# GpSimd and SyncE's queue in program order, and the values' outputs in the scores' banks: a transformer block with cached attention on one core

## Chip, cores and metric

The kernel runs on one core of one Trainium2 chip. The metric is the device time of one execution in microseconds; the median of three runs of the kernel before is 3133.72 us (3131.37 to 3137.28).

## What is computed

A block with two halves over a sequence of 2048 rows of 576 numbers, all in float32. A small vector c gives six modulation vectors (shift, gain and gate for each half).

```python
h = layernorm(x) * (1 + ca) + sa
x = x + ga * A(h)        # attention: q = h @ wq, 32 query heads of 128, 16 key/value heads
                         # k, v: the last 512 positions of two caches; softmax(q k / sqrt(128)) v, then @ wo
h = layernorm(x) * (1 + cb) + sb
x = x + gb * B(h)        # (silu(h @ w1) * (h @ w3)) @ w2, inner width 4608
```

## The kernel before

**Precision.** A matrix that goes into a matmul is split into a high half, which ScalarE casts (`fp32r`), and a low half, which another engine subtracts (`split`, L82, its lines L84 and L85). A product is then three matmuls: high by high, high by low, low by high. Low halves of weights (`wl`, `vl`, `o`) are subtracted by GpSimd (POOL in the profile), those that come from PSUM (`ql`, `ptl`, `otl`) by VectorE.

**Attention.** The sequence lies in four blocks of 512 rows (`acc`, four tiles of 128 rows each). The work is a list of 128 slots: a half of the sequence, a head, a block. The loop over slots has four steps t for each slot i, and each step issues in this order: `turn(i-1, t)` transposes a tile of the exponentials (`pt`, ScalarE's copy `pth`); `scores(i, t)` makes a tile of scores `pss`, its maximum `nm`, the low half `ptl` of the slot before, and the exponential `p`; `query(i+1, t)` does a quarter of the projection `pq` of the next slot (in the last quarter `qh` and `ql` are split off); `attend_out(i-2, t)` multiplies by `wo` and adds into `acc`; then `run(i, t)` issues the tasks that were put down for this step. After the four steps `values(i-1)` issues twelve matmuls into `po` and splits them into `oth` and `otl`. On TensorE a step is 4 + 3 + 3 + 6 matmuls (two more in the last), and `values` 12.

**Tasks.** `at(i, t, ...)` puts loads and preparations into the list of a step. For a head whose first slot is i: `load_in` (L215, L217) loads its query weights at (i-3, 1), `split_in` (L223) makes `wh` and `wl` at (i-2, 1); `load_out` (L229) loads its rows of `wo` at (i-2, 1), `gate` (L779) multiplies them by the gate on GpSimd at (i-1, 0), `split_out` (L234) splits them at (i-1, 2); the caches are loaded by `load_kv` (L239), and `split_v` (L245) stands at (i-1, 0). Three buffers (`raw`) serve all these loads.

**Weights of the second half.** Its products are done by a scheme with seven products for a 2 x 2 block of tiles, so sums and differences of weight tiles are made ahead, during the attention, split, and stored to DRAM. `load_raw` (L478, L481) loads a set, `make_set` (L490 to L499) is called seven times for it, one item a step; `load_rows` (L526) and `make_rows` (L545 to L550 in an opening call four steps ahead, then seven items through `keep`, L532 to L536) do the same for `w2`. Five items fall on four steps in the stretches where this is done. A set is loaded six steps before its first item, a pair of rows seven steps before its opening call.

**Second half.** `mlp` runs over 72 groups of seven products (L577); in each it loads the next group's weights (L570) and interleaves the matmuls of the group pair before (`down`, L643, L653, rows loaded at L565).

**PSUM.** Eight banks: `E` (two), `T` (two, later given to a second output), tag `A` (two) for `pq`, `po` and later `py`, tag `S` (two) for `pss` and later `px`.

**Order.** TensorE, VectorE and ScalarE issue in the order in which the source emits (L34, L1037). GpSimd's instructions and SyncE's, which issue nearly all transfers, are placed by the language's planner, by its own times for each instruction; all semaphores and the buffers that a tile gets are set by it too. Transfers that SyncE issues wait in its one queue.

Of the kernel before, what the change touches and what calls it, by code (L numbers as in the profile page):

```python
# [20 lines left out]
S = 2048  # L21
# [9 lines left out]
EPS = 1e-5  # L31
PB, QB, RB, HB = 4, 1, 3, 7

ORDERED = {mybir.EngineType.PE, mybir.EngineType.DVE, mybir.EngineType.Activation}  # L34
SCALE = float(DH) ** -0.5


# [1 line left out]
def tile_block(  # L39
# [28 lines left out]
    def bank(tag, name):  # L68
        return psum.tile([P, 512], F32, tag=tag, name=name)
# [12 lines left out]
    def split(hi, lo, src, eng):  # L82

        nc.scalar.copy(hi, src)  # L84
        eng.tensor_sub(lo, src, hi.bitcast(F32))  # L85
# [258 lines left out]
    def values(i):  # L344
        half, h, b = slots[i]
        st = state[i]
        vh, vl = vals[half, h // 2]
        pt = st["pt"]
        po = bank("A", "po")
        for j in range(KC):  # L350
            nc.tensor.matmul(po, vh[:, j, :], pt[0][:, j, :], start=j == 0, stop=False)  # L351
            nc.tensor.matmul(po, vl[:, j, :], pt[0][:, j, :], start=False, stop=False)  # L352
            nc.tensor.matmul(po, vh[:, j, :], pt[1][:, j, :], start=False, stop=j == KC - 1)  # L353
        oh = pool.tile([P, SB], F32R, tag="ah", name="oth", bufs=3)
        ol = pool.tile([P, SB], F32R, tag="al", name="otl", bufs=3)
        split(oh, ol, po, nc.vector)
        r = odd.tile([P, ST], F32, tag="r", name="r", bufs=3)
        nc.vector.reciprocal(r, st["l"])
        st["o"], st["r"] = (oh, ol), r
# [632 lines left out]
    for i in range(n + 2):  # L992
        run(i, -1)
        for t in range(ST):
            if 1 <= i <= n:
                turn(i - 1, t)
            if i == n:
                turn_low(i - 1, t)
            if i < n:
                scores(i, t)  # L1000
            if i + 1 < n:
                query(i + 1, t)
            if i >= m0:
                for _ in range(3 if (i, t) == (n + 1, 0) else 1):
                    next(stream)
            if 2 <= i:
                attend_out(i - 2, t)
            run(i, t)
        if 1 <= i <= n:
            values(i - 1)  # L1010
# [30 lines left out]
```

## Time and profile before

| | us |
|---|---|
| median of three runs | 3133.72 |
| span of the profiled execution (the page gives no other time of it) | 3126.2 |
| TensorE (PE) busy | 3044.8 |
| VectorE (DVE) busy | 2000.5 |
| ScalarE (ACT) busy | 1483.0 |
| GpSimd (POOL) busy | 1633.0 |

The profile is one execution on the chip. Lines such as L266 are lines of the kernel. A group of instructions is named by line, engine, operation, output and inputs. A wait "POOL oraw L779 <- DMA oraw" says which instruction waited, for whom, for how long in total, how often, and the longest. SPq is SyncE's queue of transfers, PEld TensorE's loading of weights. Matmuls are pipelined and their ends are modelled, so their durations overlap; how many start in a stretch says more than their sum. The granted clock is TensorE's, as a share of full speed.

### The profile page before, as it was taken

What the parts mean: (1) busy time and instruction counts of PE and PEld (TensorE: products, weight loads), DVE (VectorE), ACT (ScalarE), POOL (GpSimd) and SP (SyncE); (2) the same over time, 40 slices, a digit from 0 to 9 for tenths busy, and PEclk for the clock granted to TensorE, in tenths of its full rate; (3) what the DMA queues carried; (4) which work ended last, traced back from release to release, by engine and by line L of the source; (5) the groups of instructions that cost most, each with busy time, mean ns of one, the idle gap of its engine ahead of it and who ended that gap; (6) DMA issues with size and microseconds to landing.
All of it is one profiled execution on the core that took longest, in us unless ns stands there. A gap on an engine that the chain in (4) does not pass through costs nothing.

```text
span 3126.2 us, 47869 instructions
## 1 busy us (share of the span) xinstructions
PE 3044.8 (97%) x16948; PEld 2666.8 (85%) x16948; DVE 2000.5 (64%) x3042; ACT 1483.0 (47%) x3107; POOL 1633.0 (52%) x1656
## 2 busy tenths in 40 slices
PE   7999999999999999999999999999999999999998
PEld 6888877888888888888888888888888888888887
DVE  7776666666677777777767776655555555555555
ACT  5556655665565665566655553333333222222222
POOL 3357776777643762477676212345565363443444
PEclk9999999999999999999999999999999999999999
DMA  6135454545421442245544225677776776666664
GB/s 204 51 129 172 157 173 161 177 168 176 152 86 49 158 147 69 89 168 164 175 145 163 70 86 178 209 224 251 232 237 224 250 259 200 197 203 199 197 201 140
DMA packets 330128, 523.13 MB, mean 167 GB/s; under 512 B 32800, under 2 KB 161824, under 8 KB 328096
## 3 DMA queue, kind: packets, MB, share of 16 engines
q1 hardware_dynamic: 329280, 520.06, 51.1%
q8 instruction: 135, 2.21, 0.3%
q14 instruction: 105, 0.86, 0.1%
q10 hardware_dynamic: 608, 0.00, 0.0%
HBM read 369.76 MB, written 150.18 MB: 166 GB/s over the span
## 4 chain that ended last, share of the span: by engine, by line
PE 71%; POOL 5%; DMA 1%; issue 1%; DVE 1%; SPq 1%; ACT 1%; POOLq 0%; ACTq 0%; DVEq 0%
PE py L577 14%; PE px L577 11%; PE pe L282 8%; PE pq L266 6%; PE pf L653 6%; PE pe L653 6%; PE pt L335 4%; PE po L353 2%; PE po L352 2%; PE po L351 2%; PE pss L317 2%; PE pss L315 2%; PE pss L316 2%; PE pq L274 1%; POOL wmade L497 1%
## 5 line engine op out<-in xcount | busy, mean ns | idle before, releaser
L325 ACT ACTIVATE p<-pss,nm 128x512 f32<-128x512 f32 x512 | 353.2, 690 | 377.0 <-DVE nm L319 376.4
L577 PE MATMUL py<-hset,wset 128*128 128x512 f32 x2016 | 506.9, 391 | 0.0
L366 DVE SCALAR_TENSOR_TENSOR acc<-pe,r,acc 128x576 f32<-128x576 f32 x512 | 416.8, 814 | 112.1 <-PE pe L282 107.3
L319 DVE TENSOR_REDUCE nm<-pss 128x1 f32<-128x512 f32 x512 | 349.7, 683 | 123.0 <-PE pss L317 122.7
L577 PEld LDWEIGHTS py<-hset,wset 128*128 128x128 f32 x2016 | 362.5, 188 | 58.9
L577 PE MATMUL px<-hset,wset 128*128 128x512 f32 x1512 | 380.1, 391 | 0.0
L282 PEld LDWEIGHTS pe<-o,oth 128*128 128x128 f32 x2048 | 330.9, 190 | 49.6 <-DVE acc L366 7.1
L282 PE MATMUL pe<-o,oth 128*128 128x288 f32 x2048 | 359.5, 298 | 3.2 <-DVE acc L366 3.1
L342 DVE TENSOR_TENSOR ptl<-pt,pth 128x512 fp32r<-128x512 f32 x512 | 348.9, 682 | 16.3 <-ACT pth L336 15.8
L336 ACT CAST pth<-pt 128x512 fp32r<-128x512 f32 x512 | 301.1, 588 | 81.2 <-PE pt L335 77.5
L577 PEld LDWEIGHTS px<-hset,wset 128*128 128x128 f32 x1512 | 275.6, 188 | 49.4
L335 PE MATMUL pt<-ident,p 128*128 128x128 f32 x2048 | 310.9, 275 | 4.7 <-DVE ptl L342 2.6
L85 POOL TENSOR_TENSOR akv<-u,akv 128x512 fp32r<-128x512 f32 x141 | 181.5, 1297 | 241.6 <-ACT akv L84 239.0
L335 PEld LDWEIGHTS pt<-ident,p 128*128 128x128 f32 x2048 | 252.2, 142 | 18.8 <-issue 2.9
L266 PE MATMUL pq<-hT,wl 128*128 128x512 f32 x508 | 204.1, 402 | 46.0 <-POOL wl L85 45.9
L315 PE MATMUL pss<-kh,qh 128*128 128x512 f32 x512 | 246.9, 482 | 0.7 <-ACT qh L84 0.7
L85 DVE TENSOR_TENSOR otl<-po,oth 128x512 fp32r<-128x512 f32 x128 | 88.6, 692 | 228.7 <-ACT oth L84 228.7
L282 PE MATMUL pe<-o,otl 128*128 128x288 f32 x1024 | 221.0, 297 | 0.0
L84 ACT CAST oth<-po 128x512 fp32r<-128x512 f32 x128 | 75.1, 587 | 296.3 <-PE po L353 296.2
L317 PE MATMUL pss<-kh,ql 128*128 128x512 f32 x512 | 203.8, 398 | 0.0
L316 PE MATMUL pss<-kl,qh 128*128 128x512 f32 x512 | 203.7, 398 | 0.0
L497 POOL TENSOR_TENSOR wmade<-wraw,wmade 128x256 fp32r<-128x256 f32 x252 | 186.4, 740 | 32.0 <-ACT wmade L496 20.3
(181 smaller groups left out, 6533.0 us busy)
## 6 DMA issues: line engine op xcount, KB each, us to landing
oset<-od SPq DMA_DIRECT2D x106, 576.0 KB, 4.8
od<-omade SPq DMA_DIRECT2D x133, 288.0 KB, 2.7
oraw<-in_A_wo SPq DMA_DIRECT2D x64, 288.0 KB, 2.9
wraw<-in_B_w SPq DMA_DIRECT2D x144, 128.0 KB, 2.7
wraw<-in_A_wq SPq DMA_DIRECT2D x64, 256.0 KB, 2.9
w2raw<-in_B_w SPq DMA_DIRECT2D x38, 288.0 KB, 3.6
oset<-od SPq DMA_DIRECT2D x35, 288.0 KB, 3.2
wraw<-in_B_w SPq DMA_DIRECT2D x288, 32.0 KB, 2.2
```

The source lines that it names most:

```text
L85: eng.tensor_sub(lo, src, hi.bitcast(F32))
L266: nc.tensor.matmul(ps, (wh if k < 2 else wl)[:, m, :], hT[DC + m if k == 1 else m], start=s == 0, stop=False,)
L282: nc.tensor.matmul(E[:, h, :HALF], a[:, rows], b[:, h * HALF : (h + 1) * HALF], start=n == 0, stop=n == 2)
L315: nc.tensor.matmul(pss, st["qh"][:, rows], kh, start=True, stop=False)
L319: nc.vector.tensor_reduce(nm, pss, axis=AX.X, op=ALU.max, negate=True)
L325: nc.scalar.activation(p, pss, AF.Exp, bias=nm, accum_out=st["l"][:, t : t + 1])
L335: nc.tensor.transpose(ps[:, j, :], p[:, j * P : (j + 1) * P], ident)
L336: nc.scalar.copy(st["pt"][0][:, :, t * P : (t + 1) * P], ps)
L342: nc.vector.tensor_sub(pt[1][:, :, cols], state[i]["t"], pt[0][:, :, cols].bitcast(F32))
L366: nc.vector.scalar_tensor_tensor(a, E[:, :, :HALF], st["r"][:, t : t + 1], a, op0=ALU.mult, op1=ALU.add)
L577: nc.tensor.matmul(ps, w[:, a, :], h[:, b, :], start=start and n == 0, stop=stop and n == 6, skip_group_check=True)
L653: nc.tensor.matmul(ps[:, h, :HALF], a[:, rows], w[:, b, :], start=m == 0, stop=m == 2)
```

## The change

GpSimd (`Pool`) and SyncE (`SP`) join the engines that issue in the order of the source, so that all five do. And `po` is taken from the two banks of tag `S`, in turn with `pss`; the banks of tag `A` hold `pq` alone during the attention.

```diff
-ORDERED = {mybir.EngineType.PE, mybir.EngineType.DVE, mybir.EngineType.Activation}
+ORDERED = {mybir.EngineType.PE, mybir.EngineType.DVE, mybir.EngineType.Activation, mybir.EngineType.Pool, mybir.EngineType.SP}
...
-        po = bank("A", "po")
+        po = bank("S", "po")
```

## Prediction

> **What bounds the kernel now.** I read the page first, for the engine that has no room; then the waits of that engine, then the waits of whoever it waits for, then stretches of the span side by side, and last one single wait in order of time. The page:
>
> ```profile
> span 3126.2 us, 47869 instructions
> PE 3044.8 (97%) x16948; PEld 2666.8 (85%) x16948; DVE 2000.5 (64%) x3042; ACT 1483.0 (47%) x3107; POOL 1633.0 (52%) x1656
> POOL 3357776777643762477676212345565363443444
> wraw<-in_A_wq SPq DMA_DIRECT2D x64, 256.0 KB, 2.9
> ```
>
> PE is busy for 97% of the span, so nothing off PE is worth anything unless PE waits for it; 3126.2 - 3044.8 = 81.4 us is PE's idle time. GpSimd (POOL) stands at 7 tenths through most of slices 6 to 10, the stretch of the attention in which it also prepares the weights of the second half. The longest waits, "engine line waited for: total, times, longest", of PE, of POOL, and of SyncE's queue:
>
> ```profile
> PE pq L266 <- POOL wl L85: 45.9, 14, 6.6
> PE pt L186 <- DVE xn L176: 10.0, 2, 9.8
> ...
> POOL oraw L779 <- DMA oraw<-in_A_wo: 131.5, 32, 9.2
> POOL wraw L490 <- DMA wraw<-in_B_w: 99.7, 23, 7.6
> POOL w2raw L545 <- DMA w2raw<-in_B_w: 41.1, 13, 7.7
> ...
> SPq L570 <- PE py L577: 440.5, 255, 5.0
> SPq L499 <- POOL wmade L498: 352.9, 204, 10.9
> ```
>
> One wait makes up over half of PE's idle time: the queries' projection waits 14 times for the low half of its weights, which POOL subtracts. And POOL waits 272 us for loads at three lines: it stood at an instruction whose data had not come, with others ready behind it. Stretches of the span (the number behind PE's busy time counts its matmuls; the third from the end is the granted clock):
>
> ```profile
> 200.00:900.00 700.00, 659.78 (x3669) 575.05 (x3668) 462.23 (x735) 418.40 (x952) 498.75 (x608) 0.97 0.50 166
> 900.00:1000.00 100.00, 99.99 (x587) 87.77 (x586) 72.09 (x116) 62.32 (x128) 44.43 (x41) 1.00 0.18 49
> 1100.00:1200.00 100.00, 96.45 (x558) 84.05 (x557) 70.78 (x124) 59.55 (x129) 51.48 (x59) 1.00 0.38 128
> 1200.00:1500.00 300.00, 300.00 (x1723) 263.82 (x1722) 212.90 (x334) 180.22 (x402) 165.60 (x178) 1.00 0.40 131
> 1500.00:1600.00 100.00, 95.22 (x529) 82.81 (x528) 66.34 (x103) 58.71 (x133) 71.29 (x77) 0.97 0.46 152
> 1600.00:1800.00 200.00, 200.00 (x1142) 175.68 (x1141) 140.98 (x220) 115.30 (x258) 95.04 (x98) 1.00 0.38 124
> ...
> 2600.00:3000.00 400.00, 400.00 (x2177) 353.04 (x2176) 220.31 (x300) 115.86 (x203) 157.47 (x120) 1.00 0.64 200
> ```
>
> The attention's unhindered pace is (587 + 1723 + 1142) matmuls in 600 us, 5.753 a microsecond. At that pace the 3669 matmuls of 200 to 900 need 637.7 us instead of 700: 62.3 lost. 1100 to 1200 loses 3.0 and 1500 to 1600 loses 8.0. That is 73.3 us, more than the 48.5 us (40.2 + 3.5 + 4.8) of idle time in the same stretches. The rest is the clock:
>
> ```profile
> 490.00:495.00 5.00, 0.00 (x0) 0.00 (x0) 0.83 (x2) 2.11 (x5) 4.92 (x6) 0.68 0.31 120
> 495.00:500.00 5.00, 4.60 (x19) 4.23 (x20) 1.47 (x3) 0.59 (x1) 2.61 (x4) 0.64 0.60 209
> ...
> 550.00:560.00 10.00, 8.25 (x48) 6.93 (x47) 5.59 (x10) 5.18 (x12) 8.84 (x9) 1.00 0.56 188
> ```
>
> A wait of 5.58 us (shown below) is followed by a granted clock of 0.64 and 19 matmuls in 5 us; 1.75 us of idle time in 550 to 560 leaves the clock at 1.00. The second half of the kernel (2600 to 3000) has no idle time at all.
>
> **The change part by part: order.** The same wait in order of time, on POOL, SyncE's queue, ScalarE and PE:
>
> ```profile
> 478.37 1.59 POOL L533 TENSOR_TENSOR omade<-w2raw,omade 128x288 fp32r<-128x288 f32 x2
> 487.94 1.43 POOL L779 TENSOR_TENSOR oraw<-oraw,gate_a 128x576 f32<-128x576 f32 x1 [7.97 <-DMA oraw<-in_A_wo]
> 489.33 1.55 POOL L533 TENSOR_TENSOR omade<-w2raw,omade 128x288 fp32r<-128x288 f32 x2
> 490.84 0.99 POOL L490 TENSOR_TENSOR wraw<-wraw 128x384 f32<-128x384 f32 x1
> 491.91 0.99 POOL L491 TENSOR_TENSOR wraw<-wraw 128x384 f32<-128x384 f32 x1
> 492.86 0.99 POOL L493 TENSOR_TENSOR wraw<-wraw 128x384 f32<-128x384 f32 x1
> 493.81 1.53 POOL L85 TENSOR_TENSOR wl<-wraw,wh 128x640 fp32r<-128x640 f32 x1
> ```
> ```profile
> 484.28 0.37 SPq L229 DMA_DIRECT2D oraw<-in_A_wo  x1
> ```
> ```profile
> 479.73 0.71 ACT L84 CAST wh<-wraw 128x640 fp32r<-128x640 f32 x1
> ```
> ```profile
> 489.43 0.39 PE L266 MATMUL pq<-hTl,wh 128*128 128x512 f32 x1
> 495.40 0.80 PE L266 MATMUL pq<-hT,wl 128*128 128x512 f32 x1 [5.58 <-POOL wl L85]
> ```
>
> By the source this wl is written at step (i-2, 1) of its slot i, the gate L779 of the same head three steps later, at (i-1, 0), and L490, L491 and L493 belong to a weight set that is opened later still. None of the four has to stand ahead of wl; the planner put them there. The load behind the gate left only at 484.28, and POOL stood 7.97 us. ScalarE's half, the cast of wh, was over at 480.44. In program order the L533 x2 of 478.37 are followed by two more and by wl, which ends near 478.4 + 1.6 + 1.6 + 1.5 = 483.1 us, well before PE asks at 489.8. This wait goes, with its slow clock, and the same mechanism stands behind the other 13, since POOL's load waits lie in the same stretches. Value of the order: up to -73.3 us. Bounds: the idle time alone, -48.5; with the pace of the fastest clean stretch (5.87) the loss would be 74.9 + 4.9 + 9.9 = 90, so -90.
>
> **What is late next.** POOL does not get idle: the 498.75 us of work of 200 to 900 is 78% of 637.7. Two places can run late, both behind the opening batch of a row pair, which L545 to L550 issue at one step. Rows for it, and for what waits behind:
>
> ```profile
> L545 POOL TENSOR_TENSOR w2raw<-w2raw,gate_b 128x576 f32<-128x576 f32 x38 | 54.4, 1433 | 41.5 <-DMA w2raw<-in_B_w 41.1
> L547 POOL TENSOR_TENSOR w2raw<-w2raw 128x288 f32<-128x288 f32 x19 | 15.4, 811 | 1.4
> ...
> L85 POOL TENSOR_TENSOR wl<-wraw,wh 128x640 fp32r<-128x640 f32 x64 | 100.9, 1577 | 70.3 <-ACT wh L84 68.9
> L779 POOL TENSOR_TENSOR oraw<-oraw,gate_a 128x576 f32<-128x576 f32 x64 | 91.5, 1431 | 201.9 <-DMA oraw<-in_A_wo 131.5 <-PE pe L282 31.5 <-PE pt L335 19.5
> ```
>
> The batch is 2 x 1.433 + 4 x 0.811 = 6.1 us, 19 times (38 L545, two each). Between the split of wl and its first use PE has two steps, the values and part of a third step: 16 + 18 + 12 + 9 = 55 matmuls, 9.6 us. Batch, two other items (four POOL instructions at 498.75 / 608 = 0.82) and wl itself are 6.1 + 3.3 + 1.6 = 11.0, and ScalarE's cast ahead of wl comes 1 to 2 us after the step: about 3 us late, if the batch falls on one of the two steps before the split, 2 of the 8 steps of a head, so some 5 times. 0 to +15 us, taken +7. The gate: ScalarE casts the gated row two steps (32 matmuls, 5.6 us) after L779 is issued; today L779 is done early and ScalarE never waits. With the batch ahead, 6.1 + 1.4 = 7.5, so ScalarE stands 2 us, and behind it in its queue are the copies that PE's values need. 5 times 2 us, half of it in PE's sight: 0 to +10, taken +5.
>
> SyncE's queue in program order puts each store (L499, L536) behind POOL's subtraction, and the next head's loads behind that store. They are issued a slot ahead of use: 78 matmuls, 13.6 us, less 2.9 us to land, leave 10.7. Taken 0 while POOL's lag stays below that; the rival has the other case. Hoisted loads also come later, which costs nothing while they land before POOL reaches them: the lead is 6 steps for a weight set, 6 x 16 + 2 + 12 = 110 matmuls or more, 19 us. In the second half the queue already waits for PE (L570, 440.5 us over 255 times): each load there is written right after the product that frees its buffer, so the order hardly changes and the cover is 7 products. Taken 0. At the start, the third buffer of the raw tiles is waited for with the third modulation block's load behind it: bounded by the 10.0 us that PE waits there now, either way; taken +2.
>
> **The banks.** po moves from the two banks of A to the two of S. It adds an instruction nowhere. Now a po start needs the exponential of the scores two back to have read its bank:
>
> ```profile
> 968.12 0.71 ACT L325 ACTIVATE p<-pss,nm 128x512 f32<-128x512 f32 x1
> ...
> 972.22 0.39 PE L351 MATMUL po<-pth,vh 128*128 128x512 f32 x1
> ```
>
> The exponential of step 2 ends at 968.83, po starts at 972.22: 3.4 us in hand. Besides, po already waits for pth of step 3, which ScalarE does after that exponential, and the next scores already wait for qh, which ScalarE writes after the exponential of step 3. So no new wait exists; queries gain a bank they never waited for. 0; bounds: 128 slots x 0.1 us, either sign, about 13 us.
>
> Sum, from the execution's own span: 3126.2 - 73.3 + 7 + 5 + 2 = 3066.9. The page gives no time beside the span; the median of the runs, 3133.72, is 7.5 us above it, which I carry over: 3074.4, say 3075.
>
> The Trainium skill, "TensorE: Matmul & The Clock Gate", Part 1, says that an idle window of about 3.4 us halves the clock until about 3.4 us of work have passed, an estimate of 1.7 us per long wait; by it the 14 waits are worth 14 x 1.7 = 24 us beside their idle time, and the five late ones above, if each passed 3.4 us, would cost 8 us more than I took (3083). The 0.64 behind 5.58 us and the 1.00 in 550 to 560 agree.
>
> **Rivals.** (1) The wait moves: ScalarE's in-order queue takes it, as L779 now comes just in time at every head, not at five. 200 to 900 holds 637.7 / (2 x 13.6) = 23 heads; 1.5 us each is 35 us, half the gain: 3110. For it: POOL at 78%. Against: two steps are 5.6 us, and without a batch only 1.4 + 1.6 us stand ahead of it. (2) Nothing changes: PE waited because POOL has too much to do, not for its order, and the waits for loads only turn into waits for ScalarE. 3134. Against it: in 200 to 900 POOL did nothing in 700 - 498.75 = 201 us, and its three load waits sum to 272 us. (3) Slower: SyncE's queue. If POOL lags more than 10.7 us at every head, every load of a query weight comes late, since a store that waits for POOL stands ahead of it, and ScalarE's cast of wh holds the exponentials behind it. The point from which it decides is 73 / 23 = 3.2 us late at each head, a lag of 13.9 us; at 15 us it is 23 x 4.3 = 99 us, so 3160. For it: a store waits up to 10.9 us now. Against: 352.9 / 204 = 1.7 on average.
>
> **How the numbers follow.** Forecast 0.72, 3056 to 3100 by its bounds; rival 1 0.15 (3090 to 3127); rival 2 0.05; rival 3 0.08. What can be told from no change is 0.2%, 3127 to 3140: faster 0.87, same 0.05, slower 0.08. The range 3056 to 3116 leaves out rivals 2 and 3, some of rival 1 and 0.03 below.
>
> **What would show it.** Right: the waits of pq for wl gone or under 10 us; POOL's waits for the three loads near nothing, its waits for ScalarE longer; 200 to 900 at 5.7 matmuls a microsecond and a clock of 1.00; no wait of PE's po or pss for an exponential. Wrong: ScalarE waiting for L779 or for wraw by tens of microseconds, or idle time of PE in 2600 to 3000.

## Result and profile after

The changed kernel takes 3063.14 us (median of four runs, 3062.33 to 3064.24), where the kernel before ran beside it in 3133.43 us: a ratio of 0.9777 (95% interval 0.9763 to 0.9791), 70 us less. The forecast of 3075 us was 12 us too high. The page after, its first lines and GpSimd's slices:

```profile
span 3061.0 us, 47936 instructions
PE 3024.6 (99%) x16948; PEld 2652.3 (87%) x16948; DVE 2002.5 (65%) x3042; ACT 1481.6 (48%) x3107; POOL 1635.0 (53%) x1656
POOL 3267887888734731667774103345555463433344
```

Each engine does what it did before, and GpSimd is as busy as it was (1635.0 us after 1633.0). TensorE's idle time has gone from 81.4 us to 3061.0 - 3024.6 = 36.4 us. The longest waits of TensorE, and the waits of GpSimd that answer to those of before (engine, line, waited for: total, times, longest):

```profile
PE pt L186 <- DVE xn L176: 10.1, 2, 9.9
PE pe L282 <- DVE acc L366: 2.6, 4, 1.7
PE pt L335 <- DVE ptl L342: 2.6, 1, 2.6
...
POOL wl L85 <- ACT wh L84: 152.8, 40, 11.1
POOL o L85 <- ACT o L84: 141.0, 28, 13.3
...
POOL omade L533 <- ACT omade L532: 64.0, 26, 7.3
...
POOL oraw L779 <- DMA oraw<-in_A_wo: 28.5, 10, 6.0
```

The wait of pq for wl isn't in TensorE's list any more (one of 0.41 us is there under another name, see "What is late next"). GpSimd's 272 us of waits for loads at L779, L490 and L545 have become 28.5 us at L779 alone; instead it waits for ScalarE's casts, and TensorE's list shows nothing of that. The stretches of the attention in which time was lost:

```profile
200.00:900.00 700.00, 696.80 (x3984) 610.28 (x3983) 501.74 (x799) 449.69 (x1019) 528.16 (x635) 1.00 0.52 170
1100.00:1200.00 100.00, 100.00 (x591) 88.36 (x590) 71.24 (x116) 56.01 (x118) 19.92 (x21) 1.00 0.18 54
1500.00:1600.00 100.00, 100.00 (x574) 87.57 (x573) 71.05 (x111) 63.16 (x145) 79.08 (x84) 1.00 0.46 152
```

In 200 to 900 TensorE now starts 3984 matmuls instead of 3669, at a clock of 1.00 instead of 0.97. The wait that the prediction followed in order of time looks like this after, some 17 us earlier in the span, on GpSimd and TensorE:

```profile
461.53 1.58 POOL L533 TENSOR_TENSOR omade<-w2raw,omade 128x288 fp32r<-128x288 f32 x2
464.84 1.58 POOL L533 TENSOR_TENSOR omade<-w2raw,omade 128x288 fp32r<-128x288 f32 x2 [1.73 <-ACT omade L532]
467.44 1.57 POOL L85 TENSOR_TENSOR wl<-wraw,wh 128x640 fp32r<-128x640 f32 x1 [1.02 <-ACT wh L84]
...
476.11 1.44 POOL L779 TENSOR_TENSOR oraw<-oraw,gate_a 128x576 f32<-128x576 f32 x1 [2.36 <-PE pss L316]
```
```profile
476.57 0.39 PE L266 MATMUL pq<-hT,wl 128*128 128x512 f32 x1
```

The split of wl stands directly behind the two pairs of L533 and ends at 469.01; TensorE asks at 476.57, so 7.6 us are in hand where it waited 5.58 us. The gate L779 comes 8.7 us behind wl instead of ahead of it.

### The profile page after: what moved, and what is told of

Same layout as the page of the kernel before. It is cut to its first block, busy times and chain, and to the rows that moved or that the text cites. A ratio compares the mean times of both kernels' runs of the same rounds, so it can differ in the third digit from the quotient of the medians.

```text
span 3061.0 us, 47936 instructions
## 1 busy us (share of the span) xinstructions
PE 3024.6 (99%) x16948; PEld 2652.3 (87%) x16948; DVE 2002.5 (65%) x3042; ACT 1481.6 (48%) x3107; POOL 1635.0 (53%) x1656
## 4 chain that ended last, share of the span: by engine, by line
PE 93%; DVE 2%; POOL 2%; ACT 1%; issue 1%; DMA 1%; SPq 0%; ACTq 0%; POOLq 0%; DVEq 0%
PE py L577 15%; PE pe L282 13%; PE px L577 11%; PE pq L266 11%; PE pt L335 7%; PE pf L653 6%; PE pe L653 6%; PE po L353 4%; PE po L351 4%; PE po L352 4%; PE pss L317 4%; PE pss L315 4%; PE pss L316 4%; PE pq L274 2%; PE pt L252 0%
## 5 line engine op out<-in xcount | busy, mean ns | idle before, releaser
L319 DVE TENSOR_REDUCE nm<-pss 128x1 f32<-128x512 f32 x512 | 349.7, 683 | 115.5 <-PE pss L317 115.3
L497 POOL TENSOR_TENSOR wmade<-wraw,wmade 128x256 fp32r<-128x256 f32 x252 | 186.4, 740 | 79.7 <-ACT wmade L496 61.5
L84 ACT CAST oth<-po 128x512 fp32r<-128x512 f32 x128 | 75.1, 587 | 296.2 <-PE po L353 296.2
L353 PE MATMUL po<-ptl,vh 128*128 128x512 f32 x512 | 201.1, 393 | 1.2 <-DVE ptl L342 1.2
```

The source lines that it names most:

```text
L319: nc.vector.tensor_reduce(nm, pss, axis=AX.X, op=ALU.max, negate=True)
```

## Where the 65 us of span came from

The same step of the slot loop can be timed in both traces by its maximum (L319). Before minus after, the offset is -1.7 us at slot 20, 20.4 at 32, 33.9 at 48, 52.8 at 60, 57.1 at 76 and at 104, and 65.2 from 108 to the end. So 54.5 us come from slots 20 to 60, 4.3 from slots 60 to 76, 8.1 from slots 104 to 108. All of these lie in the stretches in which the second half's weights are prepared (slots 10 to 57, 66 to 75 and 85 to 117), but most of the last stretch loses nothing. In the second half of the kernel nothing moves. Of the 65.2 us, 45.0 are idle time of TensorE (81.4 - 36.4). The other 20.2 are its busy time, 3044.8 before and 3024.6 after for the same 16948 matmuls; the mean granted clock of the span goes from 0.989 to 0.997.

The prediction's estimate from the Trainium skill, "TensorE: Matmul & The Clock Gate", Part 1, was 14 x 1.7 = 24 us for the clock. The sum is near to the 20 us, but not for its reason: only six of the 14 waits are longer than 3.4 us, and in the trace of before a slower clock (0.50 to 0.68 in the next 5 us) follows eight of them, among these one of 2.16 us; behind the other six, one of them of 2.96 us, it stays at 1.00. The 5 us behind these two waits:

```profile
642.10:647.10 5.00, 4.97 (x21) 4.56 (x22) 1.83 (x3) 0.87 (x2) 4.45 (x8) 0.67 0.63 208
1148.50:1153.50 5.00, 5.00 (x31) 4.55 (x32) 2.92 (x4) 1.95 (x4) 4.53 (x7) 1.00 0.55 195
```

So the length of a wait alone doesn't tell here whether the clock falls.

## Experiments

Theory: GpSimd's order alone gives the gain, since the planner let instructions whose load had not landed stand ahead of wl. Rivals: SyncE's queue or the banks have a share; or GpSimd's amount of work is what counts. Each ratio is to the kernel before, run beside the experiment.

**Banks alone.** The kernel before, with `po` in tag `S`, and GpSimd and SyncE placed by the planner.

```diff
-        po = bank("A", "po")
+        po = bank("S", "po")
```

> Only the banks: po in the two banks of S, GpSimd and SyncE as before. Theory (order carries all): every wait that the shared banks could add is already there for another reason, so 3133 within 0.2%, waits of pq for wl about 46 us as before. Rival (banks matter): 10 us or more off the 70, 3123 or lower; or, if scores wait for the values' split, 3140 or more with a wait of pss or po in the list.

Measured: 3128.97 us, ratio to before 1.0005 (0.9994 to 1.0015). TensorE's waits are those of before:

```profile
PE pq L266 <- POOL wl L85: 44.6, 13, 6.8
```

The banks are worth nothing that can be measured.

**Order alone.** The changed kernel with `po` back in tag `A`.

```diff
-        po = bank("S", "po")
+        po = bank("A", "po")
```

> Only the order: GpSimd and SyncE in program order, po in the banks of A as before. Theory: the whole gain, 3063 within 0.2%. Rival (banks matter): above 3073.

Measured: 3063.45 us, ratio 0.979 (0.9771 to 0.9809). All of the gain is the order's.

**GpSimd's order alone.** The kernel before with GpSimd in program order; SyncE's queue is placed by the planner.

```diff
-ORDERED = {mybir.EngineType.PE, mybir.EngineType.DVE, mybir.EngineType.Activation}
+ORDERED = {mybir.EngineType.PE, mybir.EngineType.DVE, mybir.EngineType.Activation, mybir.EngineType.Pool}
```

> GpSimd alone in program order, SyncE's transfers left to the planner, po in A. Theory (GpSimd stood at hoisted instructions whose loads had not come): with its own order put right nothing stands ahead of wl, 3063 to 3070, waits for wl under 5 us. Rival (SyncE's order is the cause: loads sent late behind stores): the gain stays away, 3110 or more, and GpSimd still waits for loads by over 200 us.

Measured: 3063.36 us, ratio 0.9787 (0.977 to 0.9803), with 3999 matmuls in 200 to 900. GpSimd's instructions stand in the same order as in the changed kernel, and SyncE's 2012 transfers in the order of before at all but 49 places, so this run separates the two. With the loads placed by the planner GpSimd doesn't wait for one at L779 at all, so the 28.5 us of such waits after are the price of SyncE's program order; the times show nothing of it (3063.36 against 3063.45). Ordering GpSimd is enough.

**SyncE's order alone.** The kernel before with SyncE in program order; GpSimd is placed by the planner.

```diff
-ORDERED = {mybir.EngineType.PE, mybir.EngineType.DVE, mybir.EngineType.Activation}
+ORDERED = {mybir.EngineType.PE, mybir.EngineType.DVE, mybir.EngineType.Activation, mybir.EngineType.SP}
```

> SyncE alone in program order, GpSimd left to the planner, po in A. Theory: the hoisted gate now stands ahead of wl while its load is written only beside wl, and stores that wait for GpSimd stand ahead of that load, so GpSimd waits as long or longer for loads: 3130 to 3200, waits for wl 45 us or more. Rival (SyncE's order is the cause): 3063 to 3085.

Measured: 3069.67 us, ratio 0.9809 (0.9793 to 0.9824). I expected no gain or a loss, and it brings 58 of the 65 us, within the range that the rival gave (3063 to 3085). GpSimd's and TensorE's waits:

```profile
POOL wraw L490 <- DMA wraw<-in_B_w: 74.6, 26, 7.5
POOL oraw L779 <- DMA oraw<-in_A_wo: 69.9, 25, 7.2
POOL w2raw L545 <- DMA w2raw<-in_B_w: 7.1, 4, 3.6
```
```profile
PE pq L266 <- POOL wl L85: 4.7, 5, 2.3
```

The planner, given another order of the transfers, also placed GpSimd's instructions otherwise. Counted in the list of GpSimd's instructions, a gate L779 stands on average ahead of 2.6 instructions that come before it in the source, at most 8; before it was 8.6, at most 20. L490 does so for 6.8 instead of 17.0. A gate that the source has later stands ahead of wl at 18 of the 64 heads; before it was 61. So this run isn't a case of GpSimd's old order with a new queue: the 272 us of waits for loads fell to 152, and the waits for wl from 45.9 us to 4.7. The last experiment shows that the gain doesn't need SyncE's order; that GpSimd's order is what mattered here too agrees with these counts, but a run with the old order of GpSimd pinned under SyncE's new one was not made, so that isn't shown.

**The gate ahead of wl in the source.** All five engines in program order, but in the source the gate stands right behind its load, ahead of the split of wl.

```diff
         if i >= 2:
             at(i - 3, 1, load, wqs, key, load_in, wq, h * DH)
+            if i > 2:
+                at(i - 2, 1, load, wos, key, load_out, wo, h * DH)
+                at(i - 2, 1, gate, wos, key, "a")
             at(i - 2, 1, put, wqs, key, split_in)
-        at(*(i - 2, 1) if i > 2 else (0, -1), load, wos, key, load_out, wo, h * DH)
-        at(*(i - 1, 0) if i > 2 else (1, 1), gate, wos, key, "a")
+        if i <= 2:
+            at(0, -1, load, wos, key, load_out, wo, h * DH)
+            at(1, 1, gate, wos, key, "a")
```

> The changed kernel with the gate L779 written at (i-2, 1), right behind its own load and ahead of the split of wl: an instruction that waits for its load stands ahead of wl, in program order. Theory (GpSimd standing at a load is what made wl late): GpSimd waits 3 to 5 us for the load at each of 62 heads, 200 to 300 us in all, wl comes that much later; with 9.6 us to its use that is late only where work is queued besides: 3065 to 3090. Rival (program order of SyncE's queue cures it, whatever GpSimd's order): 3063 within 0.2%, and GpSimd's waits for oraw below 100 us.

Measured: 3196.83 us, ratio 1.0215 (1.0199 to 1.023): 134 us more than the changed kernel, and more than the kernel before. There, too, a gate stood ahead of wl at 61 of the 64 heads, but the gates waited 131.5 us for their loads, and here they wait 252.0.

```profile
POOL oraw L779 <- DMA oraw<-in_A_wo: 252.0, 40, 12.5
```
```profile
PE pq L266 <- POOL wl L85: 83.0, 21, 9.2
```

The mechanism can so be made at will: one instruction that waits for a transfer, ahead of wl. I expected 3065 to 3090, a fifth of the loss at most, since I counted only a few us of landing, and GpSimd stands up to 12.5 us. That the load is itself queued behind stores that wait for GpSimd would account for it; no run takes that apart.

**All opening sums early as well.** As the last, and the opening sums of a weight set (L490, L491, L493, in a call of their own) five steps and those of a row pair (L545 to L550) six steps earlier, one step behind their loads.

```diff
-        if n == 0:
+        if n < 0:
             nc.gpsimd.tensor_add(s1, a21, a22)
             nc.gpsimd.tensor_sub(s2, s1, a11)
+            nc.gpsimd.tensor_sub(a21, a11, a21)
+            return
         elif n == 2:
-            nc.gpsimd.tensor_sub(a21, a11, a21)
...
-            if maker is make_rows:
-                at((step - 4) // 4, (step - 4) % 4, maker, w, -1)
+            early_step = step - (5 if maker is make_set else 10)
+            at(early_step // 4, early_step % 4, maker, w, -1)
```

> As the kernel with the gate first, and besides the opening sums of a weight set (L490, L491, L493) and of a row pair are written one step behind their loads, five and six steps earlier than in the changed kernel: about the order that the planner had chosen for GpSimd, with SyncE in program order. Theory (that order of GpSimd makes the loss, with either order of the queue): GpSimd waits over 300 us for loads and much of the loss is back, 3095 to 3170, with waits of pq for wl of 25 us or more. Rival (with the queue in program order the loads come in time): 3063 to 3075.

Measured: 3248.6 us, ratio 1.0377 (1.0359 to 1.0394), above the 3095 to 3170 that I expected, and two long groups of waits for loads:

```profile
POOL oraw L780 <- DMA oraw<-in_A_wo: 177.9, 40, 12.5
POOL wraw L489 <- DMA wraw<-in_B_w: 169.0, 28, 8.1
```
```profile
PE pq L266 <- POOL wl L85: 104.1, 23, 14.0
```

Program order brings nothing by itself: a source that is written in this order costs 185 us against the changed kernel.

**Less lead for wl.** The split moves from two steps and the values ahead of its use to the last step ahead of it.

```diff
-            at(i - 2, 1, put, wqs, key, split_in)
+            at(i - 2, 3, put, wqs, key, split_in)
```

> The changed kernel with the split of the query weights two steps later, at (i-2, 3): between split and first use lie 12 + 9 = 21 matmuls, 3.7 us, instead of 55, 9.6 us. This measures how far GpSimd is behind its place in the source. If it is 3 us behind at ordinary heads, as the prediction took for five of them, wl comes 2 to 4 us late at most of the 64 heads and the time is 3120 to 3180; if it is rarely behind, only ScalarE's cast and the 1.6 us of wl itself count, waits of about 0.5 us, 3063 to 3090.

Measured: 3081.4 us, ratio 0.9845 (0.983 to 0.9859).

```profile
PE pq L266 <- POOL wl L85: 17.2, 6, 5.1
```

Six waits, at 226, 284, 343, 402, 464 and 1364 us, and each stands behind an opening batch. The first of them on GpSimd, with its batch:

```profile
214.43 1.44 POOL L545 TENSOR_TENSOR w2raw<-w2raw,gate_b 128x576 f32<-128x576 f32 x1
215.82 0.81 POOL L546 TENSOR_TENSOR w2raw<-w2raw 128x288 f32<-128x288 f32 x1
...
218.37 0.81 POOL L550 TENSOR_TENSOR w2raw<-w2raw 128x288 f32<-128x288 f32 x1
219.13 0.74 POOL L497 TENSOR_TENSOR wmade<-wraw,wmade 128x256 fp32r<-128x256 f32 x1
...
224.56 1.55 POOL L85 TENSOR_TENSOR wl<-wraw,wh 128x640 fp32r<-128x640 f32 x1
```

The place is the one that the prediction gave for its residual, behind the batch. The lead taken away is 55 - 21 = 34 matmuls, 34 / 5.753 = 5.9 us, and the longest wait is 5.1 us, from which I took it that the worst head of the changed kernel has 0.8 us in hand. That doesn't follow: the longest wait, at 464, is at a head whose wl ends 5.4 us ahead of its use in the changed kernel, where that batch stands behind the split. The changed kernel's own trace has the margins (below, "What is late next"): the tightest heads have nothing in hand.

**The query weights' load late.** Issued two steps ahead of the cast, instead of a slot.

```diff
-            at(i - 3, 1, load, wqs, key, load_in, wq, h * DH)
+            at(i - 2, -1, load, wqs, key, load_in, wq, h * DH)
```

> The changed kernel with the load of the query weights written at (i-2, -1) instead of (i-3, 1): two steps (32 matmuls, 5.6 us) before ScalarE's cast, of which landing takes 3.3. It measures how far SyncE's queue is behind its place when a store that waits for GpSimd stands ahead of a load. Rival 3 of the prediction (queue more than 10 us behind at every head): each of some 57 heads waits 8 us or more, 3300 and above. If it is behind by its mean wait at a store, about 2 us: ScalarE waits for wraw 10 to 60 us in all, 3063 to 3090.

Measured: 3179.4 us, ratio 1.0157 (1.014 to 1.0174), well above what I expected.

```profile
ACT wh L84 <- DMA wraw<-in_A_wq: 128.5, 31, 11.5
```
```profile
PE pe L282 <- DVE acc L366: 86.8, 28, 9.7
```

ScalarE's cast of wh stands for its load at 31 heads, 128.5 / 31 = 4.1 us on average, and the exponentials, the split outputs and at last TensorE stand behind it. Two steps are 5.6 us, of which 3.3 are for landing: a load that is 4.1 us late has been held up in the queue by some 5.6 - 3.3 + 4.1 = 6.4 us in this run, an estimate from these rows. So the third rival's mechanism, a load that comes late through the queue, is there. That its price (116 us) is near the rival's 99 us is chance: the rival counted 23 heads behind a lag of 15 us, here it is 31 heads, a lag of about 6.4 us and a shorter lead. The lead of a slot just covers it: in the changed kernel half of these loads land 7.8 us or more ahead of the cast, but at slots 24 and 38 the cast starts as the load lands.

**Twice the larger subtraction, and twice the smaller.** Is it GpSimd's amount of work? L497 issued twice adds 183 us to its busy time (1817.9 after 1635.0), L498 issued twice 113 us (1748.3). Both write the same values again.

```diff
         nc.gpsimd.tensor_sub(t[:, 3:, :], x[:, :2, :], t[:, :2, :].bitcast(F32))
+        nc.gpsimd.tensor_sub(t[:, 3:, :], x[:, :2, :], t[:, :2, :].bitcast(F32))
```
```diff
         nc.gpsimd.tensor_sub(t[DR:, 2, :], x[DR:, 2, :], t[DR:, 2, :].bitcast(F32))
+        nc.gpsimd.tensor_sub(t[DR:, 2, :], x[DR:, 2, :], t[DR:, 2, :].bitcast(F32))
```

> The changed kernel with the 128x256 subtraction of each item (L497) done twice: 252 x 0.74 = 186 us more on GpSimd, about 130 of them in 200 to 900, where it then works 94% of the time instead of 75%. Theory (order, not load, made PE wait; GpSimd has a fifth of its time free): at 94% the opening batches no longer drain and part of the loss returns, 3070 to 3105. Rival (GpSimd's load was the cause and the change only made room): the whole loss returns, 3130 or more.

> The changed kernel with the 64x128 subtraction of each item (L498) done twice: 252 x 0.46 = 116 us more on GpSimd, some 80 of them in 200 to 900. If GpSimd's free time is a margin that is used up first (75% busy in 200 to 900 becomes 87%), most of this is absorbed: 3065 to 3095. If each us of its work costs PE (3181 with 186 us more, 0.63 us a us): 3137.

Measured: 3181.3 us (ratio 1.0163, 1.0148 to 1.0178) and 3125.66 us (0.9986, 0.9977 to 0.9996). Both expectations missed: the smaller addition takes back nearly the whole gain, and the larger lands where its rival had put it (GpSimd's load as the cause, 3130 or more). That rival can't be the cause of the gain, since GpSimd's busy time is the same before and after (1633.0 and 1635.0 us); but the load is close to where it takes the gain back. TensorE's and ScalarE's waits with the larger one:

```profile
PE pq L266 <- POOL wl L85: 34.9, 8, 6.6
PE po L351 <- ACT pth L336: 34.7, 13, 8.0
```
```profile
ACT o L84 <- POOL oraw L780: 39.1, 11, 8.8
ACT omade L533 <- POOL w2raw L549: 33.4, 11, 4.7
```

(A line more ahead of it moves L779 to L780.) This is the first rival's wait, ScalarE behind the gate, and it appears once GpSimd has too much to do. I then formed the theory that the price is paid at the opening batch, where I took 0.8 us to be in hand.

**The batch spread.** The opening sums of a row pair fall on four steps, in the kernel with the smaller subtraction doubled, and in the changed kernel with nothing doubled.

```diff
-            for j in range(2):
+            if n < -2:
+                j = n + 4
                 r = whole[:, 2 * j : 2 * j + 2, :]
                 nc.gpsimd.tensor_mul(r, r, half_split(gates["b"]))
-            nc.gpsimd.tensor_sub(t1, b12, b11)
-            nc.gpsimd.tensor_sub(t2, b22, t1)
-            nc.gpsimd.tensor_sub(t4, b21, t2)
-            if p != LAST:
-                nc.gpsimd.tensor_sub(b12, b22, b12)
+            elif n == -2:
+                nc.gpsimd.tensor_sub(t1, b12, b11)
+                nc.gpsimd.tensor_sub(t2, b22, t1)
+            else:
+                nc.gpsimd.tensor_sub(t4, b21, t2)
+                if p != LAST:
+                    nc.gpsimd.tensor_sub(b12, b22, b12)
...
-                at((step - 4) // 4, (step - 4) % 4, maker, w, -1)
+                for part in range(-4, 0):
+                    at((step - 3 + part) // 4, (step - 3 + part) % 4, maker, w, part)
```

> The changed kernel with the second half of the subtraction for the gated weights (L498) issued twice, as in e10, but with the opening sums of a pair of rows spread over the four steps before they are read (one share each), where e10 issues them all at one step. GpSimd has the same 116 us more as in e10, and otherwise the same instructions. Theory (the price of e10 was paid at the batch: 0.8 us of margin behind it, so that what is added ahead of each batch comes through): TensorE waits for wl and pth go from 36 us to under 10 us, and the time is 3065 to 3090 us. Rival (the amount of GpSimd work sets the price, wherever it stands): it stays at 3115 to 3135 us.

> The changed kernel with the opening sums of a pair of rows spread over four steps, and nothing doubled. Theory (no wait of TensorE for GpSimd is left in the changed kernel, so there is nothing for more margin to remove): 3063 us within 0.3%, and no wait for wl. Rival (the batch still delays something that the list of waits does not name, such as the granted clock): 3045 to 3055 us.

Measured: 3122.16 us (ratio 0.9983, 0.9973 to 0.9993) with the work doubled, against 3125.66 with the batch in one piece: the theory of the batch fell, the amount of work sets the price. Without doubling 3062.19 us (0.979, 0.9773 to 0.9807), the changed kernel's time: there was next to nothing left to remove, and no version beats it by more than 1 us. Three stretches of GpSimd in the kernel doubled and spread, the busy time in the fifth place after the length:

```profile
399.00:425.00 26.00, 23.30 (x130) 19.66 (x129) 16.06 (x25) 14.54 (x33) 24.04 (x35) 1.00 0.31 111
425.00:444.00 19.00, 19.00 (x112) 16.68 (x111) 13.53 (x22) 12.46 (x29) 13.81 (x16) 1.00 0.78 243
444.00:484.00 40.00, 37.17 (x206) 31.82 (x205) 25.69 (x40) 23.29 (x54) 36.96 (x53) 0.98 0.43 143
```

And the corresponding ones of the changed kernel:

```profile
375.00:400.00 25.00, 25.00 (x145) 21.95 (x143) 17.97 (x28) 15.70 (x37) 23.44 (x29) 1.00 0.40 139
400.00:419.00 19.00, 19.00 (x107) 16.58 (x106) 13.01 (x21) 11.33 (x27) 13.41 (x17) 1.00 0.81 252
419.00:445.00 26.00, 26.00 (x151) 22.95 (x150) 18.95 (x30) 18.14 (x41) 19.66 (x26) 1.00 0.51 171
```

While sets are made, GpSimd is full: 24.04 of 26 us and 36.96 of 40. What is missing to the whole, 2.0 and 3.0 us, are pauses of at most 0.15 us between instructions (see the last section). While rows are made, it waits for ScalarE's casts and can't use the time. In the changed kernel the stretch of the sets is full at its end alone (23.44 of 25), and has room at its start (19.66 of 26).

The prices of the two doublings fit this. From slot 12 to slot 56, which take 612.0 us in the changed kernel, the kernel with the smaller doubling loses 50.9 us against the changed one (45.7 with the batch spread), and the kernel with the larger doubling 89.8. L497 and L498 stand there some 146 times each, so between the two doublings lie 146 x (0.74 - 0.46) = 41 us of GpSimd's work and 89.8 - 50.9 = 39 us of time: there each further microsecond of GpSimd costs about a whole one. The smaller doubling itself adds 146 x (0.46 + 0.08) = 79 us and costs 51 (46 spread), so by this estimate the changed kernel has some 28 to 33 us of room in those slots, about 5%.

## The prediction, step by step

**Value of the order** (-73.3 us): right in its mechanism, its place and nearly its size. The kernels with one part each show that GpSimd's order carries it, and the gate put ahead of wl makes the wait at will. By the offsets of slots it is worth 54.5 + 4.3 + 8.1 = 67 us. The pace was set too high: I took 5.753 matmuls a microsecond from the clean stretches of before; 200 to 900 now runs, with 3.2 us of idle time, at 3984 / 700 = 5.69. By that pace the same rows give 700 - 3669 / 5.69 = 55.2 for that term instead of 62.3, in line with the 54.5.

**What is late next** (+7 for wl, +5 for the gate): the place was right, the size was not, and it is the largest error of the sum. The batch stands ahead of the split, with at most three items between, at slots 14, 18, 22, 52, 56 and 88, six heads where I said some five. But wl is late at one of them only, by 0.4 us. ScalarE, GpSimd and TensorE at slot 22:

```profile
326.97 0.71 ACT L84 CAST wh<-wraw 128x640 fp32r<-128x640 f32 x1
```
```profile
329.78 2.84 POOL L545 TENSOR_TENSOR w2raw<-w2raw,gate_b 128x576 f32<-128x576 f32 x2
...
335.87 1.56 POOL L85 TENSOR_TENSOR wl<-wraw,wh 128x640 fp32r<-128x640 f32 x1
```
```profile
326.60 0.42 PE L282 MATMUL pe<-o,otl 128*128 128x288 f32 x2
...
337.49 0.50 PE L266 MATMUL pq<-hT,wl 128*128 128x512 f32 x1 [0.41 <-DVE nm L319]
```

The wait is put down to nm, which ended last (337.48), but wl ended only at 337.43, and the loading of TensorE's weights (PEld) had waited for it. So the list of waits hides it. At slot 18 wl ends 0.1 us ahead of its use, at slot 14 1.6 us. I had 11.0 us of queued work, a cast of 1 to 2 us ahead of it and a lead of 9.6 us, and so 3 us too late. From the end of the step (327.02) to the end of wl there are 10.4 us, against a lead of 10.1 (327.02 to 337.08): the cast, over at 327.68, ran beside GpSimd's work and not ahead of it, and the lead was longer. ScalarE waits for the gate twice, 3.3 us in all (ACT o L84 <- POOL oraw L779).

**SyncE's queue** (0): right, and closer than I said: at two heads the load of the query weights lands only as its cast starts. 28.5 us of waits at the gate are its price, hidden; two steps of lead instead of a slot would have cost 116 us.

**The banks** (0, bounds 13 us either way): right, 1.0005 (0.9994 to 1.0015), and the order without them takes the time of the order with them. No wait of po or pss for an exponential appeared.

**The start** (+2): within the 1.8 us that the offset at slots 0 to 20 shows (the load of a cache, 2.1 us, is a part of it). **Second half** (0): right; from the first product into py to the last it takes 1227.3 us before (1878.7 to 3106.0) and 1227.7 us after (1813.5 to 3041.2).

**What lies around the span** (+7.5): wrong. The profiled execution after took 3062.74 us for a span of 3061.0, 1.7 us more, and the kernel with the banks alone 3131.66 for 3129.9. So the 7.5 us were no time around the span: the profiled execution of before must have taken about 3128, one of its faster ones. The error of 12 us is then 6 from here and 12 from the residuals (14 taken, about 2 found), less 6 by which the order's value was set too high. That they cancel in part is luck. And the 3056 to 3100 that the prediction names "by its bounds" is narrower than its bounds: -90 us with nothing late leads to 3126.2 - 90 + 7.5 = 3044, and -48.5 with 15 and 10 us late to 3110.

**Rivals.** The first (ScalarE waits) and the third (the queue) didn't come, but both are real: the doubled subtraction brings the one, the late load the other. The second, that GpSimd has too much work, was nearer than its argument says. I set GpSimd's 201 us without work in 200 to 900 against it. After, GpSimd is without work for 124.5 us of slots 12 to 56 (busy 487.5 of 612.0); by the estimate above only some 30 us of these can be used, and 113 us more work over the whole kernel takes back nearly the whole gain.

## What to carry to other kernels

When an engine waits for a load with ready work behind it, and that work is what the bottleneck waits for, look at the order in which the two stand and pin the order of that one engine; whether the source's order is a good one is a question of its own (the same pinning with the gate written early cost 134 us). Judge the room on such an engine by short stretches with no waits in them, not by its share of busy time: here 487.5 us of 612 left room for about 30 more, by the estimate above. Where a wait is put down to one engine, look whether another ended just before it. And take the time around the span from a run whose own time is known, not from the median.

## Not expected of the hardware

GpSimd's busy time leaves out a pause between some of its instructions: between L497 and L498 it is 0.08 us in the mean of 152 pairs in 200 to 900. The group's row in the changed kernel has it as idle time without a releaser (19.8 us over 252):

```profile
L498 POOL TENSOR_TENSOR wmade<-wraw,wmade 64x128 fp32r<-64x128 f32 x252 | 116.1, 461 | 19.8
```

A subtraction of 0.46 us so occupies GpSimd for 0.54 us. An engine that shows 24.04 of 26 us busy, as above, is full.
